# Delta-rule attention in front of two MoE layers: key-query products and state updates over four quarters of the array

## The chip, the cores and the metric

One core of one Trainium2 chip runs the whole program. The metric is the device time of one execution in microseconds. Three runs of the kernel before took 1043.93, 1046.31 and 1048.43 us; the median is 1046.31 us.

## The reference

Attention has 4 batches, 8 heads, 768 tokens and head size 48. Each head carries a 48x48 state that every token updates by a delta rule:

```python
k_n = k / (np.linalg.norm(k, axis=-1, keepdims=True) + 1e-06)
state = np.zeros((B, H, D, D), dtype=np.float32)
for t in range(S):
    kt, vt, bt = (k_n[:, :, t], v[:, :, t], beta[:, :, t, None])
    y[:, :, t] = np.einsum('bhd,bhde->bhe', q[:, :, t], state)
    v_old = np.einsum('bhde,bhd->bhe', state, kt)
    state = state + bt[:, :, :, None] * np.einsum('bhd,bhe->bhde', kt, vt - v_old)
```

The result, turned to 3072 tokens of 384 numbers, goes through two layers of the form `act(x @ w_in) @ w_out` with 2048 hidden units: an ELU in the first, `h * sigmoid(1.702 h)` in the second. All in float32.

## The kernel before, in words

**Chunks.** The tokens of a head are cut into 12 chunks of 64. Within a chunk the recurrence is solved in closed form: a Gram matrix of the keys (`gram`, L174) is inverted as a triangular system (`inverse`, `join16`, and `t2`, `m1`, `m2` in `chunk`), and the rest is small matrix products per head. `chunk(c)` (L331) returns these steps by name: `kq` (products of keys and queries, 64x64 per head, L352), `mask` (their strict causal part, L368), `ks` (keys times the old state, L414), `w` (the inverse applied to the values less that, L430), `state` (the new state, L451), `y` (the output, L464) and `out` (a transpose into the tiles that the first MoE layer reads, L486).

**Where the heads lie.** There are 32 pairs of batch and head. They are named by `hf` (0 or 1), `ab` (0 or 1) and `u` (0 to 7). `tok(ab)` is the partition half (0 to 63 or 64 to 127) in which the tokens of a head lie for `ks`, `w` and `y`. `w_half(hf, ab)`, called `k`, is `ab` for `hf` 0 and `1 - ab` for `hf` 1. The tiles `x[k]` and `su[k]` each hold two things: for `x[k]`, queries (48 rows) in half `1 - k` and the masked key-query products in half `k`; for `su[k]`, the state in half `1 - k` and the result of `w` in half `k`. So `y` is one product over all 128 partitions.

**Which part of the array a product uses.** The rows of the array are the partitions of the operands, its columns the partitions of the output. Before the change, `kq` reads half `1 - k` and writes half `k` (L359 to L365), and `state` reads half `k` and writes half `1 - k` (L456 to L459): both use two of the four quarters of 64x64, in turn by `turns()` (L105). `ks` reads half `1 - k` and writes half `ab` (L420 to L426), and `w` reads half `ab` and writes half `k` (L438 to L443), both by `order()` (L100).

**VectorE behind them.** `mask` (L377) multiplies the products, read from PSUM, by a 0/1 mask into `x[k]`: two operations of 64x1024 a chunk, or four of 64x512 for chunk 0, whose products lie in two separate PSUM tiles. `state` (L462) adds its product, read from PSUM, to the state into the other copy `nx[k]`: two operations of 48x768.

**Order of the work.** Everything is in program order on each engine. Chunks 0 and 1 run in a hand-written order ahead of the MoE work (L744 to L811). After that the program runs through units of the first MoE layer, 9 matmuls `up` (L576) and 9 matmuls `down` (L610) of 128x512 each; tables of slots (L829 to L867) say at which unit and at which of three places in it each step of a chunk is issued. `mask` is issued right behind its `kq` from chunk 2 on. A step costs the table a due share of VectorE (`VECTOR`, L943), which sets how the inverse of later chunks and the splitting of weights (`prep`, L541 to L555) are spread. All of `kq`, `ks`, `w`, `state`, `y`, `gram` and `out` take the one PSUM tile `ps_w` of two banks (`wide`, L118, one buffer), so each waits until the one before has been read out. In chunks 0 and 1 some take the banks of the MoE accumulators instead.

The DMA issues all stand on SyncE's queue, and none belongs to the changed steps.

Of the kernel before, what the change touches and what calls it, by code (L numbers as in the profile page):

```python
# [14 lines left out]
ALU = mybir.AluOpType  # L15
PSUM = bass.MemoryType.PSUM

B, H, S, D = 4, 8, 768, 48
# [9 lines left out]
HB = D * H  # L28
# [3 lines left out]
class Kernel:  # L32
# [67 lines left out]
    def order():  # L100

        return [(hf, ab) for hf in range(2) for ab in range(2)]

    @staticmethod
    def turns():  # L105

        return [(0, 0), (0, 1), (1, 1), (1, 0)]

    @staticmethod
    def tok(ab):  # L110
# [220 lines left out]
    def chunk(self, c):  # L331

        nc, ap = self.nc, self.ap
        v, pe, act, pool = nc.vector, nc.tensor, nc.scalar, nc.gpsimd
        first, last = c == 0, c == NC - 1
        s = self.pas[c // 2]
        us = slice(16 * (c % 2), 16 * (c % 2) + 16)
        su = [self.su[k, c % 2] for k in range(2)]
        nx = [self.su[k, 1 - c % 2] for k in range(2)]
        g = self.grp.setdefault(c, {})  # L340
        st = {}

        def hs(u):
            return slice(u * D, (u + 1) * D)
# [7 lines left out]
        def kq():  # L352
            if first:
                ps = self.banks(0)
            else:
                both = self.wide()
                ps = [both[:, hf] for hf in range(2)]
            for u in range(8):
                for hf, ab in self.turns():  # L359
                    k = self.w_half(hf, ab)  # L360
                    r = 64 * (1 - k)
                    pe.matmul(  # L362
                        ps[hf][self.tok(k), 64 * u:64 * u + 64], g["kt"][r:r + D, 8 * hf + u, :],
                        g["x"][k][r:r + D, 8 * hf + u, :], start=True, stop=True,
                    )  # L365
            st["kq"] = ps if first else both

        def mask():  # L368
            ps = st.pop("kq")
            for k in range(2):  # L370
                r = self.tok(k)
                for f, part in (((0, ps[0]), (1, ps[1])) if first else ((None, ps),)):
                    if f is None:
                        o, i = g["x"][k][r], part[r].rearrange("p f (u t) -> p (f u) t", u=8)
                    else:
                        o, i = g["x"][k][r, 8 * f:8 * f + 8], part[r].rearrange("p (u t) -> p u t", u=8)
                    v.tensor_tensor(  # L377
                        out=o, in0=i, in1=self.mask_p[r].unsqueeze(1).to_broadcast(list(i.shape)), op=ALU.mult,
                    )

        def t2():
            st["t2"] = self.place(c, "t2")
# [68 lines left out]
        def state():  # L451
            if last:
                return
            ps = self.wide()
            for u in range(8):
                for hf, ab in self.turns():  # L456
                    k = self.w_half(hf, ab)
                    t, r = self.tok(k), slice(64 * (1 - k), 64 * (1 - k) + D)
                    pe.matmul(ps[r, hf, hs(u)], g["kn"][t, hf, hs(u)], su[k][t, hf, hs(u)], start=True, stop=True)  # L459
            for k in range(2):  # L460
                r = slice(64 * (1 - k), 64 * (1 - k) + D)
                v.tensor_tensor(out=nx[k][r], in0=su[k][r], in1=ps[r, :, 0:HB], op=ALU.add)  # L462

        def y():  # L464
            st["y"] = ap.tile([P, 2, HB], F32, name="y", tag="ry", bufs=2)
# [20 lines left out]
        def out():  # L486
# [10 lines left out]
            for i in range(2):  # L497
# [4 lines left out]
                v.tensor_tensor(out=xl[:, :, dst], in0=src, in1=xh[:, :, dst].bitcast(F32), op=ALU.subtract)  # L502

        return dict(nv=nv, t2=t2, m1=m1, kq=kq, mask=mask, m2=m2, ks=ks, w=w, state=state, y=y, out=out)

    def x_tiles(self, key):
# [536 lines left out]
```

## Time and profile before

| what | value |
|---|---|
| runs | 1043.93, 1046.31, 1048.43 us |
| span of the profiled execution | 1047.7 us; no other time of this execution is given |
| TensorE busy | 996.2 us (95%), 12136 matmul rows |
| VectorE busy | 591.2 us (56%), 1021 instructions |
| ScalarE busy | 453.4 us (43%) |
| attention's work | from the start to about 570 us |

A product of two float32 operands shows as two matmul rows in the profile, so a step over 32 heads shows as x64 for one chunk. "PEld" is the weight load of TensorE, which runs beside its matmuls. "PEclk" is the granted TensorE clock in tenths of full speed. "Idle before" in square brackets is the time for which the engine stood idle ahead of that row, with what ended it; "issue" is a wait for nothing that the profile shows.

### The profile page before, as it was taken

Reading aid. Unit: us, or ns where it says so; the run is one execution under the profiler, and the core shown is the slowest. Engines: PE = TensorE matmul, PEld = TensorE weight load, DVE = VectorE, ACT = ScalarE, POOL = GpSimd, SP = SyncE. Lnnn points to the kernel's source line nnn. Section 1 sums busy time; section 2 is a strip of 40 time slices with the busy share of each in tenths; the row PEclk is TensorE's granted clock in tenths of the full one; section 3 lists DMA queues with packets and bytes.
Section 4 is the critical chain, followed back from the end, with each engine's and each line's share of the span. In section 5 each row is a group of like instructions: output and inputs, shape, how many; then the busy total and the mean of one; then the engine's idle time right before and its main releaser. Section 6 shows DMA issues by size and latency. Waiting matters only on the chain.

```text
span 1047.7 us, 26839 instructions
## 1 busy us (share of the span) xinstructions
PE 996.2 (95%) x12136; PEld 854.1 (82%) x12136; DVE 591.2 (56%) x1021; ACT 453.4 (43%) x749; POOL 49.5 (5%) x65
## 2 busy tenths in 40 slices
PE   2678898999999999999999999999999999999998
PEld 2666776877788888888888788999999999999997
DVE  5579568837786777668434676743333333333333
ACT  1254575544445445545544766533333333333322
POOL 2000000000001000000000010000100001000000
PEclk9677999999999999999999999999999999999999
DMA  5252341401220221211001741001010010010000
GB/s 178 114 174 97 114 153 53 132 34 61 63 91 20 72 77 53 71 39 65 18 17 61 281 201 61 1 1 61 1 53 9 1 61 1 23 38 1 31 1 31
DMA packets 20178, 68.40 MB, mean 65 GB/s; under 512 B 3168, under 2 KB 6240, under 8 KB 20064
## 3 DMA queue, kind: packets, MB, share of 16 engines
q1 hardware_dynamic: 20064, 66.69, 18.7%
q8 instruction: 95, 1.56, 0.6%
q14 instruction: 19, 0.16, 0.0%
HBM read 57.25 MB, written 9.44 MB: 64 GB/s over the span
## 4 chain that ended last, share of the span: by engine, by line
PE 92%; DVE 4%; issue 2%; DMA 1%; ACT 1%; SPq 0%; ACTq 0%; DVEq 0%
PE h L576 38%; PE acc L610 18%; PE acc L621 10%; PE accn L621 10%; PE ps_w L362 2%; PE ps_w L474 2%; PE ps_w L459 2%; PE ps_w L188 2%; PE ps_b L392 1%; PE ps_b L407 1%; PE ps_w L423 1%; DMA kg<-in_kT 1%; PE ps_w L440 1%; PE ps_w L496 1%; PE ps_b L323 1%
## 5 line engine op out<-in xcount | busy, mean ns | idle before, releaser
L576 PE MATMUL h<-xh,wt 128*128 128x512 f32 x1152 | 401.0, 402 | 6.4 <-DVE wt L555 5.0
L576 PEld LDWEIGHTS h<-xh,wt 128*128 128x128 f32 x1152 | 219.5, 191 | 53.2 <-DVE wt L555 6.3
L576 PE MATMUL h<-xl,wt 128*128 128x512 f32 x576 | 229.4, 398 | 0.0
L610 PE MATMUL acc<-gh,wt 128*128 128x512 f32 x576 | 197.0, 396 | 0.5 <-DVE xo L674 0.5
L598 ACT CAST gh<-t 128x512 fp32r<-128x512 f32 x192 | 119.2, 621 | 174.8 <-DVE t L589 118.7
L601 DVE TENSOR_TENSOR gl<-t,gh 128x512 fp32r<-128x512 f32 x192 | 138.7, 723 | 68.1 <-PE acc L621 30.9
L595 DVE TENSOR_TENSOR t<-t,h 128x512 f32<-128x512 f32 x96 | 66.0, 688 | 180.3 <-ACT t L592 180.2
L592 ACT ACTIVATE t<-h 128x512 f32<-128x512 f32 x96 | 57.4, 598 | 198.9 <-PE h L576 198.9
L610 PEld LDWEIGHTS acc<-gh,wt 128*128 128x128 f32 x576 | 108.9, 189 | 24.4 <-issue 0.9
L576 PEld LDWEIGHTS h<-xl,wt 128*128 128x128 f32 x576 | 109.8, 191 | 19.2 <-DVE xl L502 0.2
L610 PE MATMUL acc<-gl,wt 128*128 128x512 f32 x288 | 112.9, 392 | 0.0
L589 DVE SCALAR_TENSOR_TENSOR t<-t,h 128x512 f32<-128x512 f32 x96 | 65.6, 684 | 76.2 <-ACT t L586 75.7
L585 ACT ACTIVATE t<-h 128x512 f32<-128x512 f32 x96 | 57.4, 598 | 113.5 <-PE h L576 112.8
L621 PE MATMUL acc<-wt,gh 128*128 128x384 f32 x384 | 98.5, 337 | 0.0
L621 PE MATMUL accn<-wt,gh 128*128 128x384 f32 x384 | 98.1, 336 | 0.0
L621 PEld LDWEIGHTS accn<-wt,gh 128*128 128x128 f32 x384 | 71.0, 188 | 5.4
L621 PEld LDWEIGHTS acc<-wt,gh 128*128 128x128 f32 x384 | 70.3, 188 | 2.8
L621 PE MATMUL acc<-wt,gl 128*128 128x384 f32 x192 | 64.9, 338 | 0.0
L621 PE MATMUL accn<-wt,gl 128*128 128x384 f32 x192 | 64.8, 337 | 0.0
L610 PEld LDWEIGHTS acc<-gl,wt 128*128 128x128 f32 x288 | 54.4, 189 | 10.3
L586 ACT ACTIVATE t<-t 128x512 f32<-128x512 f32 x96 | 60.6, 632 | 3.0
L640 POOL TENSOR_TENSOR xl<-x1r,xh 128x512 fp32r<-128x512 f32 x18 | 24.4, 1355 | 413.9 <-ACT xh L639 321.8
(143 smaller groups left out, 968.7 us busy)
## 6 DMA issues: line engine op xcount, KB each, us to landing
raw<-in_w SPq DMA_DIRECT2D x32, 768.0 KB, 7.4
kt<-in_kT SPq DMA_DIRECT2D x12, 512.0 KB, 4.6
x<-in_qT SPq DMA_DIRECT2D x24, 256.0 KB, 4.2
kg<-in_kT SPq DMA_DIRECT2D x10, 512.0 KB, 4.7
vn<-in_vn SPq DMA_DIRECT2D x12, 384.0 KB, 4.3
kn<-in_kn SPq DMA_DIRECT2D x12, 384.0 KB, 3.6
x1d<-xo SPq DMA_DIRECT2D x12, 384.0 KB, 2.9
x1r<-x1d SPq DMA_DIRECT2D x6, 768.0 KB, 4.6
```

What stands on the lines that cost most here:

```text
L188: self.nc.tensor.matmul(o[q:q + 32], k[:, 32 * sub:32 * sub + 32], x, start=True, stop=True)
L576: nc.tensor.matmul(hps, wt[:, part, k * P:(k + 1) * P], src[:, k, c], start=(i == 0), stop=(i == 3 * NK - 1))
L585: nc.scalar.activation(out=t, in_=hps, func=AF.Relu, scale=-1.0)
L586: nc.scalar.activation(out=t, in_=t, func=AF.Exp, scale=-1.0)
L589: nc.vector.scalar_tensor_tensor(out=t, in0=t, scalar=-1.0, in1=hps, op0=ALU.add, op1=ALU.max)
L592: nc.scalar.activation(out=t, in_=hps, func=AF.Sigmoid, scale=1.702)
L595: nc.vector.tensor_tensor(out=t, in0=t, in1=hps, op=ALU.mult)
L598: nc.scalar.copy(gh, t)
L601: nc.vector.tensor_tensor(out=gl, in0=t, in1=gh.bitcast(F32), op=ALU.subtract)
L610: self.nc.tensor.matmul(acc[c], wt[:, part, DM + c * P:DM + (c + 1) * P], src, start=(m == 0 and i == 0), stop=(m == NM - 1 and i == 2),)
L621: self.nc.tensor.matmul(acc[w], src[:, c], wt[:, part, DM:2 * DM], start=(m == 0 and i == 0), stop=(m == NM - 1 and i == 2),)
L640: nc.gpsimd.tensor_tensor(out=xl, in0=raw, in1=xh.bitcast(F32), op=ALU.subtract)
```

## The change

`kq` writes half `ab` in place of half `k`, and `state` writes half `1 - ab` in place of `1 - k`; both go through the heads by `order()`. Operands stay where they were. So each of the two steps uses all four quarters of the array. For `hf` 1 the result now lies in the other partition half from where it belongs, and the VectorE operation that reads it from PSUM writes it to its half. As the halves of `hf` 0 and 1 no longer go together, `mask` and the state's addition become four operations each. `turns()` is gone.

```diff
--- before.py
+++ after.py
@@ -100,11 +100,6 @@
     def order():
 
         return [(hf, ab) for hf in range(2) for ab in range(2)]
-
-    @staticmethod
-    def turns():
-
-        return [(0, 0), (0, 1), (1, 1), (1, 0)]
 
     @staticmethod
     def tok(ab):
@@ -356,27 +351,24 @@
                 both = self.wide()
                 ps = [both[:, hf] for hf in range(2)]
             for u in range(8):
-                for hf, ab in self.turns():
+                for hf, ab in self.order():
                     k = self.w_half(hf, ab)
                     r = 64 * (1 - k)
                     pe.matmul(
-                        ps[hf][self.tok(k), 64 * u:64 * u + 64], g["kt"][r:r + D, 8 * hf + u, :],
+                        ps[hf][self.tok(ab), 64 * u:64 * u + 64], g["kt"][r:r + D, 8 * hf + u, :],
                         g["x"][k][r:r + D, 8 * hf + u, :], start=True, stop=True,
                     )
-            st["kq"] = ps if first else both
+            st["kq"] = ps
 
         def mask():
             ps = st.pop("kq")
-            for k in range(2):
-                r = self.tok(k)
-                for f, part in (((0, ps[0]), (1, ps[1])) if first else ((None, ps),)):
-                    if f is None:
-                        o, i = g["x"][k][r], part[r].rearrange("p f (u t) -> p (f u) t", u=8)
-                    else:
-                        o, i = g["x"][k][r, 8 * f:8 * f + 8], part[r].rearrange("p (u t) -> p u t", u=8)
-                    v.tensor_tensor(
-                        out=o, in0=i, in1=self.mask_p[r].unsqueeze(1).to_broadcast(list(i.shape)), op=ALU.mult,
-                    )
+            for hf, ab in self.order():
+                k, t = self.w_half(hf, ab), self.tok(ab)
+                i = ps[hf][t].rearrange("p (u t) -> p u t", u=8)
+                v.tensor_tensor(
+                    out=g["x"][k][self.tok(k), 8 * hf:8 * hf + 8], in0=i,
+                    in1=self.mask_p[t].unsqueeze(1).to_broadcast(list(i.shape)), op=ALU.mult,
+                )
 
         def t2():
             st["t2"] = self.place(c, "t2")
@@ -453,13 +445,14 @@
                 return
             ps = self.wide()
             for u in range(8):
-                for hf, ab in self.turns():
+                for hf, ab in self.order():
                     k = self.w_half(hf, ab)
-                    t, r = self.tok(k), slice(64 * (1 - k), 64 * (1 - k) + D)
+                    t, r = self.tok(k), slice(64 * (1 - ab), 64 * (1 - ab) + D)
                     pe.matmul(ps[r, hf, hs(u)], g["kn"][t, hf, hs(u)], su[k][t, hf, hs(u)], start=True, stop=True)
-            for k in range(2):
-                r = slice(64 * (1 - k), 64 * (1 - k) + D)
-                v.tensor_tensor(out=nx[k][r], in0=su[k][r], in1=ps[r, :, 0:HB], op=ALU.add)
+            for hf, ab in self.order():
+                k = self.w_half(hf, ab)
+                r, q = [slice(64 * (1 - x), 64 * (1 - x) + D) for x in (k, ab)]
+                v.tensor_tensor(out=nx[k][r, hf], in0=su[k][r, hf], in1=ps[q, hf, 0:HB], op=ALU.add)
 
         def y():
             st["y"] = ap.tile([P, 2, HB], F32, name="y", tag="ry", bufs=2)
```

## Rows read from the trace of the kernel before

**Rows 1.** The page, parts 1 and 2: busy time, and granted clock in 40 slices.
```profile
PE 996.2 (95%) x12136; PEld 854.1 (82%) x12136; DVE 591.2 (56%) x1021; ACT 453.4 (43%) x749; POOL 49.5 (5%) x65
...
PEclk9677999999999999999999999999999999999999
```

**Rows 2.** Stages: stretch, length, busy PE, PEld, DVE, ACT, POOL; clock, DMA share, GB/s.
```profile
0.00:75.00 75.00, 43.37 (x1804) 39.84 (x1804) 44.06 (x97) 22.88 (x41) 9.30 (x22) 0.82 0.48 157
75.00:179.00 104.00, 90.63 (x1881) 71.80 (x1882) 79.16 (x127) 57.27 (x97) 3.65 (x6) 0.90 0.33 109
179.00:570.00 391.00, 388.51 (x6121) 319.10 (x6122) 258.67 (x507) 183.89 (x303) 12.11 (x19) 0.99 0.18 55
570.00:1047.00 477.00, 473.72 (x2333) 423.38 (x2331) 209.30 (x292) 189.31 (x310) 24.39 (x18) 1.00 0.13 50
```

**Rows 3.** Timeline of TensorE, full clock: start, length, line, out<-in, shape, count.
```profile
364.48 1.64 PE L459 MATMUL ps_w<-su,kn 64*48 64x48 f32 x64
...
375.11 2.08 PE L362 MATMUL ps_w<-x,kt 48*64 48x64 f32 x64
...
396.57 1.49 PE L188 MATMUL ps_w<-kg 48*32 48x64 f32 x128
...
422.09 1.15 PE L423 MATMUL ps_w<-su,kt 48*64 48x48 f32 x64
...
428.60 1.15 PE L440 MATMUL ps_w<-r,z 64*64 64x48 f32 x64
```

**Rows 4.** Timeline of VectorE: masks, state additions, and copies of half the width.
```profile
45.84 2.57 DVE L377 TENSOR_TENSOR x<-acc,mask_p 64x512 f32<-64x512 f32 x4
...
61.32 1.92 DVE L462 TENSOR_TENSOR su<-su,ps_w 48x768 f32<-48x768 f32 x2 [2.17 <-PE ps_w L459]
...
69.54 1.12 DVE L447 COPY su<-acc 64x384 f32<-64x384 f32 x2 [0.54 <-PE acc L440]
```

**Rows 5.** Waits by total, count and longest; then timeline rows of the PSUM buffer.
```profile
DVE x L377 <- PE ps_w L362: 16.3, 10, 3.0
DVE su L462 <- PE ps_w L459: 16.0, 10, 3.0
...
238.39 1.15 PE L423 MATMUL ps_w<-su,kt 48*64 48x48 f32 x64 [0.38 <-DVE x L377]
...
377.24 2.47 DVE L377 TENSOR_TENSOR x<-ps_w,mask_p 64x1024 f32<-64x1024 f32 x2 [1.11 <-PE ps_w L362]
...
381.43 2.07 PE L474 MATMUL ps_w<-su,x 128*64 128x48 f32 x64
```

**Rows 6.** TensorE before 100 us: three bursts, and the stage of one.
```profile
54.75 1.95 PE L440 MATMUL acc<-vn,z 64*64 64x48 f32 x62 [0.24 <-ACT z L412]
...
58.47 2.80 PE L459 MATMUL ps_w<-su,kn 64*48 64x48 f32 x64
...
94.13 3.68 PE L362 MATMUL ps_w<-x,kt 48*64 48x64 f32 x64
...
94.00:98.00 4.00, 4.00 (x66) 3.75 (x66) 2.91 (x5) 1.95 (x3) 0.00 (x0) 0.50 0.86 291
```

**Rows 7.** The chain of waits (start, length, what), and a DMA queue of the page.
```profile
34.80 1.84 issue
...
123.75 1.78 PE ps_w L362 x56
125.53 0.86 issue
...
q8 instruction: 95, 1.56, 0.6%
```

**Rows 8.** Timeline of TensorE and VectorE where VectorE's chain comes between.
```profile
90.85 1.22 PE L576 MATMUL h<-xh,wt 128*128 128x512 f32 x2 [3.68 <-DVE wt L555]
...
152.21 1.92 DVE L462 TENSOR_TENSOR su<-su,ps_w 48x768 f32<-48x768 f32 x2 [1.26 <-PE ps_w L459]
...
178.93 1.51 PE L496 MATMUL ps_w<-ident,y 128*128 128x128 f32 x6 [2.64 <-DVE su L462]
```

## The prediction, made before the change was run

> **What bounds the kernel now.** I read the page first. TensorE is busy 95% of the span, and its granted clock is at the upper of its two levels (2.4 GHz) in most slices after the first fifth [rows 1]. A kernel like that gets shorter by what TensorE no longer has to do, but only in stretches where TensorE is what ends last. So I then cut the span into stages [rows 2]. From 179 to 570 us TensorE is busy 388.5 of 391 us, VectorE 258.7: here TensorE alone sets the pace. From 75 to 179 us TensorE is busy 90.6 of 104 us and VectorE 79.2: the two take turns. Before 75 us TensorE is busy 43.4 of 75 us: waits rule. After 570 us the attention is over and nothing of the change runs.
>
> The third view is the timeline of TensorE at the full clock, where a burst is read off whole [rows 3]. All bursts below have 64 matmul rows (32 products, two rows each), except the Gram product with 128. The two that the change touches are the slow ones: the key-query burst takes 2.08 us and the state burst 1.64 us, both in two quarters of the array. The key-state product (L423) and the w product (L440) take 1.15 us; their code goes through all four quarters, L423 in the very order that the changed key-query products take. So the trace of before already holds the changed form's price. There are 12 key-query bursts (chunks 0 to 11) and 11 state bursts (chunks 0 to 10).
>
> **TensorE's part.** The key-query product keeps its 64 stationary columns, as L423 has them, and streams 64 columns where L423 streams 48. The Gram product streams 64 too and needs only 1.49 us for 128 rows [rows 3], so the streamed columns do not seem to set the pace. I take 1.15 us; the bad end is 1.15 x 64/48 = 1.53 us. Saved: 0.93 us a burst (0.55 to 0.93). The state product has 48 stationary columns, between the Gram product's 32 (1.49/128 = 11.6 ns a row) and L423's 64 (18.0 ns). Halfway is 14.8 ns, so 0.95 us (ends: 0.75 and 1.15). Saved: 0.69 us (0.49 to 0.89).
>
> **The order against the rule.** The changed order within a unit visits the row halves as B, A, A, B, so every second row has its predecessor in the same half. L440 goes A, B, A, B and L423 goes B, A, A, B, and both take 1.15 us [rows 3]: the order costs nothing there. The Trainium skill, "TensorE: Matmul & The Clock Gate", Part 3 (Packing small matmuls), says that a weight load overlaps running matmuls only when it goes to another row group. By that rule about half of the loads would be exposed, and the sum below would be about half as large; the equal rows speak against it.
>
> **VectorE's part.** Two masks of 64x1024 become four of 64x512. The first chunk has that form already: four in 2.57 us, against 2.47 us for two wide ones [rows 4]. That adds 0.10 us a chunk. Two state additions of 48x768 (1.92 us) become four of 48x384. The nearest row is a pair of 64x384 copies from PSUM at 1.12 us, so four take 2.24 us: 0.32 us more. New is also that half of these operations write to the partition half that they don't read from. No row shows that. I take no extra cost, because the nearest rows are the same shapes within a half. It may not gain, since the element count per partition is unchanged; as its bad end I take four times the time, which is the third rival below. In the stage after 179 us the extra time is covered: VectorE mostly stands waiting for just these bursts, 10 times each for 16.3 and 16.0 us [rows 5], so it begins earlier when they end earlier. And the single PSUM buffer that mask and addition must free is next wanted later: the mask that starts at 377.24 ends at 379.71, while the next user starts at 381.43 [rows 5]. Where VectorE is the bound, the cover is gone and the 0.10 or 0.32 us counts. Chunk 0's mask has four operations either way. No DMA is moved and the program order of the pieces stays.
>
> **The sum, burst by burst.**
> - After 179 us, 8 key-query bursts (chunks 4 to 11) and 7 state bursts (chunks 4 to 10): 8 x 0.93 + 7 x 0.69 = 12.3 us. At chunk 4 the key-state product already waits 0.38 us for the mask [rows 5], so the mask's 0.10 us counts there.
> - Key-query of chunk 2, at 94 us, runs at the lower clock level (0.50 granted in 94 to 98 us) and takes 3.68 us. The w product at that level takes 1.95 us for 62 rows, 2.0 us for 64 [rows 6]. TensorE works on without waiting behind it, so 1.7 us are saved.
> - State of chunk 0, at 58 us, takes 2.80 us at the lower level [rows 6]; I take 1.8 us, so 1.0 us is saved (0 to 1.2). Behind it TensorE has work in a row.
> - Key-query of chunks 0 and 1: nothing (0 to 2.8 us). They are followed by a stall of 1.84 us in which TensorE waits for nothing that the profile shows [rows 7]. Such stalls come back after each 128 or so dense matmuls with as many weight loads. The queue of kind "instruction" carries 95 packets in 1.56 MB [rows 7], 16.4 KB each. I read this as code arriving in blocks; the block that ends that stall would not come sooner because TensorE ran out of the previous one sooner. Key-query of chunk 3 is broken by such a stall after 56 of its rows [rows 7]: nothing either (0 to 0.9).
> - State of chunk 1: VectorE follows it and TensorE waits 3.68 us for the weights that VectorE splits [rows 8]. The burst's gain goes into that wait, and VectorE's addition lies on the path: a loss of about 0.15 us.
> - State of chunks 2 and 3: the addition of chunk 2 starts right behind the burst, and from there VectorE is the chain until TensorE has waited 2.64 us for the addition of chunk 3 [rows 8]. Gained 0.69 at the head, lost 0.32 twice, and the second burst's gain ends in the wait: nothing.
>
> Together: 12.3 - 0.1 + 1.7 + 1.0 - 0.15 = 14.7 us. The profiled span is 1047.7 us; its execution has no separate time, so I count nothing around the span. It lies 1.4 us above the median of the runs, 1046.31, and inside their spread. 1047.7 - 14.7 = 1033.0, and against the median 1031.6; I forecast 1032 us.
>
> **The rivals.**
> - Half of it. Successive rows in one row half block each other, so half run at the pace of the two-quarter burst. Key-query 1.62 us, state 1.30 us: 8 x 0.46 + 7 x 0.34 + 1.3 for the early ones less 0.25 = 7.2 us, so 1039 us. For it: I infer the mechanism of the slow pace from few shapes, and none is 64 by 64 in four quarters. Against it: L423 and L440 [rows 3]. Chance 0.13. The skill's rule above is this rival.
> - The change doesn't do what it says: the quarters still run one after the other for these operands. Then only VectorE's additions count, 0.32 three times and 0.10 once, so 1047 us. Chance 0.06.
> - Slower: writing to the other partition half is slow on VectorE. If such an operation takes four times the others' 0.64 and 0.56 us, a mask takes 6.4 us and an addition 5.6 us. Between the burst's end and the next user of the buffer some 4.2 us pass [rows 5], so four masks would stall TensorE 2.2 us each, chunk 4's about 3.9, seven additions 1.4 each, and the three additions on VectorE's own stretches [rows 8] add 3.7 each: 33.6 us against 14.7 gained, 1065 us. At three times it costs 16.5 us and breaks even; from there it decides. Nothing in the trace speaks for or against it but the steady price per element of all VectorE rows. Chance 0.05.
> - More: the early key-query bursts gain as well, since the code blocks are asked for earlier: 14.7 + 2.8 + 0.9, so 1028 us. Chance 0.06.
>
> **How the numbers follow.** The forecast keeps 0.70. Its own range: with 1.53 us for key-query and 1.15 us for state, and nothing at chunk 0, the gain is 9 us; with 0.75 us for state and the early bursts, 20 us: 1026 to 1037 us. The runs of before lie 2 us to either side of their median. With the half rival the range is 1025 to 1040 us. About 0.5% (5.2 us) is what a measurement of this kernel can tell from no change; faster than 1041 us are the forecast, the greater gain and most of the half rival: 0.87. Same: the quarters that don't overlap and the rest: 0.08. Slower: 0.05.
>
> **What would show it.** In the profile after, the key-query burst at 1.15 us and the state burst near 0.95 us at the full clock; four masks in about 2.6 us and four additions in about 2.25 us, those that cross halves as long as the others; TensorE's busy time in the stage after 179 us down by some 12 us with no new waits on L377 or L462; the stalls at 35 and 125 us still there and longer; the wait for the addition of chunk 3 still near 2.6 us. The prediction is wrong if the bursts keep a pace above 25 ns a row, if crossing operations are longer, or if new waits of TensorE of over a microsecond drop its clock to the lower level where it was at the upper.

## The result and the profile after

The changed kernel takes 1035.78 us (median of four runs, 1033.48 to 1037.44) against 1046.57 us for the kernel before in the same session (median of four, 1043.93 to 1048.43). Over all these runs the ratio is 0.9893, 95% interval 0.9872 to 0.9914. Run again as it is, beside other kernels, it came to 0.9882 (0.9860 to 0.9905). So it is 11 to 12 us faster. The forecast was 1032 us, 14.7 us faster; the range of 1025 to 1040 us held.

The page of the profiled execution, its span and part 1, to be read against [rows 1]:

```profile
span 1035.7 us, 26881 instructions
...
PE 982.5 (95%) x12136; PEld 837.4 (81%) x12136; DVE 598.6 (58%) x1065; ACT 453.2 (44%) x749; POOL 49.2 (5%) x65
```

TensorE has as many matmuls as before and is busy 13.7 us less. VectorE has 44 instructions more (two more masks and two more additions for each of 11 chunks) and 7.4 us more to do.

Line numbers move with the diff: L362 is now L357, L377 is L368, L459 is L451, L462 is L455. TensorE's bursts at the full clock, in the timeline (start, length, line, out<-in), against [rows 3]:

```profile
359.82 0.94 PE L451 MATMUL ps_w<-su,kn 64*48 64x48 f32 x64
...
369.74 1.16 PE L357 MATMUL ps_w<-x,kt 48*64 48x64 f32 x64
```

The state burst went from 1.64 to 0.94 us and the key-query burst from 2.08 to 1.16 us.

VectorE's new operations, first all of a line (count, shortest/median/longest in ns), then one group of four in the timeline for each, against [rows 4]:

```profile
L368 DVE TENSOR_TENSOR x<-ps_w,mask_p x44: 676/690/695, 50.3 to 547.1; 64x512 f32<-64x512 f32 x44
...
L455 DVE TENSOR_TENSOR su<-su,ps_w x44: 545/553/558, 58.7 to 515.4; 48x384 f32<-48x384 f32 x44
...
370.97 2.80 DVE L368 TENSOR_TENSOR x<-ps_w,mask_p 64x512 f32<-64x512 f32 x4 [0.20 <-PE ps_w L357]
...
427.79 2.25 DVE L455 TENSOR_TENSOR su<-su,ps_w 48x384 f32<-48x384 f32 x4 [0.95 <-PE ps_w L451]
```

In each group of four, the last two write to the other partition half. In the mask group shown the four last 684, 695, 683 and 695 ns, and between the shortest and the longest of a line lie 19 and 13 ns. So an operation that crosses is not longer than one that doesn't.

Four masks take 2.80 us (2.47 before), four additions 2.25 us (1.92 before). Not all of that is the cutting into four. The kernel called VectorE's split only, described below, has the same shapes, all within their own half, and its groups are shorter:

```profile
373.96 2.62 DVE L377 TENSOR_TENSOR x<-ps_w,mask_p 64x512 f32<-64x512 f32 x4 [1.10 <-PE ps_w L362]
...
432.38 2.05 DVE L463 TENSOR_TENSOR su<-su,ps_w 48x384 f32<-48x384 f32 x4 [1.64 <-PE ps_w L459]
```

There two masks of one half follow each other, and the second starts 0.61 us after the first, before that has ended; where the half changes it is 0.70 us. In the changed kernel the half that is read changes with every operation, and every step is 0.70 to 0.71 us, also between the first two, neither of which crosses. So about 0.2 us of each group goes by the order of the operations, not by the crossing.

The waits in total, against the first two of [rows 5]:

```profile
DVE su L455 <- PE ps_w L451: 9.1, 9, 2.3
DVE x L368 <- PE ps_w L357: 7.6, 9, 2.7
PE ps_w L489 <- DVE su L455: 3.6, 1, 3.6
PE ps_w L415 <- DVE x L368: 0.7, 1, 0.7
```

VectorE stood 16.3 and 16.0 us waiting for these bursts; now it is 7.6 and 9.1 us. That idle time is what the added instructions and the shorter bursts were taken from. TensorE's own waits for them grew from 2.64 to 3.65 us at the addition of chunk 3 and from 0.38 to 0.74 us at the mask of chunk 4.

**Where the 12 us came from.** One mark that all kernels share is the start of chunk 4's key-query burst. In the profile before, then after:

```profile
233.66 2.08 PE L362 MATMUL ps_w<-x,kt 48*64 48x64 f32 x64
```

```profile
233.58 1.16 PE L357 MATMUL ps_w<-x,kt 48*64 48x64 f32 x64
```

Up to there the two profiled executions are level. From there to the end of the span it is 1047.7 - 233.66 = 814.0 us before and 1035.7 - 233.58 = 802.1 us after: 11.9 us, all of it behind the mark.

### The profile page after: what moved, and what is told of

The parts are those of the page before. It is cut to its first block, busy times and chain, and to the rows that moved or that the text cites. A ratio compares the mean times of both kernels' runs of the same rounds, so it can differ in the third digit from the quotient of the medians.

```text
span 1035.7 us, 26881 instructions
## 1 busy us (share of the span) xinstructions
PE 982.5 (95%) x12136; PEld 837.4 (81%) x12136; DVE 598.6 (58%) x1065; ACT 453.2 (44%) x749; POOL 49.2 (5%) x65
## 4 chain that ended last, share of the span: by engine, by line
PE 90%; DVE 5%; issue 2%; DMA 1%; ACT 1%; SPq 0%; ACTq 0%
PE h L569 39%; PE acc L603 19%; PE acc L614 10%; PE accn L614 10%; PE ps_w L467 2%; PE ps_w L357 1%; PE ps_w L183 1%; PE ps_b L399 1%; PE ps_b L384 1%; PE ps_w L415 1%; PE ps_w L432 1%; PE ps_w L451 1%; PE ps_w L489 1%; PE ps_b L310 1%; PE ps_b L318 1%
```

## The experiments

Three questions were open: do the late bursts carry the whole gain; what became of the 1.7 + 1.0 - 0.15 = 2.55 us forecast for the chunks before 179 us; and why are four quarters faster. In the table, "rest" is the span less the start of chunk 4's key-query burst, and the ratio is that to the kernel before, run in the same session.

| kernel | ratio and 95% interval | burst of chunk 4 starts | rest |
|---|---|---|---|
| before (profile shown above) | 1 | 233.66 | 814.0 |
| changed | 0.9893 (0.9872 to 0.9914) | 233.58 | 802.1 |
| changed, again | 0.9882 (0.9860 to 0.9905) | 232.02 | 801.9 |
| key-query only | 0.9933 (0.9909 to 0.9957) | 235.37 | 807.5 |
| state only | 0.9965 (0.9946 to 0.9984) | 231.08 | 808.8 |
| VectorE's split only | 1.0013 (0.9997 to 1.0029) | 230.69 | 813.8 |
| chunks 4 to 11 only | 0.9878 (0.9861 to 0.9895) | 232.19 | 801.9 |
| chunks 0 to 3 only | 1.0012 (0.9996 to 1.0028) | 233.58 | 814.4 |
| chunk 3's key-query as before | 0.9875 (0.9855 to 0.9895) | 229.49 | 802.4 |
| chunk 3's key-query moved | 0.9880 (0.9854 to 0.9906) | 226.68 | 801.8 |
| row halves alternate | 0.9879 (0.9858 to 0.9899) | 231.94 | 802.2 |

**The parts.** Key-query only keeps the old state update, state only the old key-query products and masks:

```diff
 def kq():
-  for hf, ab in self.turns():  ... ps[hf][self.tok(k), ...]
+  for hf, ab in self.order():  ... ps[hf][self.tok(ab), ...]
```

> Only the key-query products take four quarters and four masks; the state update stays as before. Theory A: 8 bursts after 179 us save 0.92 us each, 7.4 us, and the early chunks lose about 2 us through the longer stall and the clock: 1040 to 1042 us. Rival V (VectorE's added instructions eat the gain): under 3 us gained, over 1043 us, with new waits of TensorE for the mask beyond the one of chunk 4.

Measured: 0.9933, 7 us of the 1046.57; the rest is 6.5 us shorter. In the forecast's terms it should be 8 x 0.92 less the 0.36 us that the mask of chunk 4 costs, 7.0 us; the missing 0.5 us was not traced. Rival V, under 3 us gained, is out.

```diff
 def state():
-  for hf, ab in self.turns():  ... slice(64 * (1 - k), 64 * (1 - k) + D)
+  for hf, ab in self.order():  ... slice(64 * (1 - ab), 64 * (1 - ab) + D)
```

> Only the state update takes four quarters and four additions; the key-query products stay as before. Theory A: 7 bursts after 179 us save 0.70 us each, 4.9 us, chunk 0 up to 1 us, and chunk 3's key-query stall stays at 0.9 us without a fall of the clock: 1040 to 1042 us. Rival V (VectorE's added instructions eat the gain): over 1043.5 us, with longer waits of TensorE for the additions.

Measured: 0.9965, 3.7 us (1.7 to 5.7); the rest is 5.2 us shorter, against 7 x 0.70 = 4.9. The median is 1042.96 us beside 1048.39 us for the kernel before in that session, and the interval reaches into the expected gain of 4.6 to 6.6 us without covering it. The late part is as expected; what the early part gave can't be told from these runs. The two parts' rests add to 11.7 us, the changed kernel's 11.9.

**VectorE's share alone.** The products stay in two quarters, and masks and additions are only cut into four:

```diff
-  for f, part in (((0, ps[0]), (1, ps[1])) if first else ((None, ps),)):
+  for f, part in ((0, ps[0]), (1, ps[1])):
...
-  v.tensor_tensor(out=nx[k][r], in0=su[k][r], in1=ps[r, :, 0:HB], op=ALU.add)
+  for hf in range(2):
+      v.tensor_tensor(out=nx[k][r, hf], in0=su[k][r, hf], in1=ps[r, hf, 0:HB], op=ALU.add)
```

> Both products stay in two quarters as before; only VectorE's masks and additions are split into four, all within their own half. This is VectorE's part of the change alone. Theory A: the extra 0.3 us an addition and 0.3 us a mask are hidden but for chunks 1 to 4: 0 to 1.5 us slower than before, 1046 to 1048 us. Rival V: 3 us or more slower, 1049 to 1051 us.

Measured: 1.0013 (0.9997 to 1.0029), and a rest of 813.8 us, as before. The cost is hidden in the late stretch. In all, the interval runs from 0.3 us faster to 3.0 us slower, so Rival V is just at its end. The operations of this kernel stay in their half, so it does not hold the 0.2 us a group that the changed order adds.

**The early chunks.** The profile after shows the key-query burst of chunk 3 cut by a stall, as in [rows 7], and a slow stretch behind it. First the burst in the timeline, then pieces of the chain of waits (start, length, what), then the stretch as a whole (as in [rows 2], the clock is the third number from the end):

```profile
121.15 1.04 PE L357 MATMUL ps_w<-x,kt 48*64 48x64 f32 x56
...
123.88 0.49 PE L357 MATMUL ps_w<-x,kt 48*64 48x64 f32 x8 [1.69 <-issue]
```

```profile
124.38 4.14 PE acc L603 x9
...
130.36 3.81 PE h L569 x9
...
135.30 2.28 PE acc L603 x9
```

```profile
124.00:134.00 10.00, 10.00 (x90) 7.56 (x90) 6.97 (x10) 2.77 (x5) 0.00 (x0) 0.52 0.10 16
```

The 56 rows ahead of the stall went from 1.85 to 1.04 us, and the stall from 0.86 to 1.69 us: what the burst saved, the stall took. Then nine long matmuls took 4.14 and 3.81 us, where at the upper clock level they take 2.28. Before, this stretch ran at the upper level. The first theory was therefore that the longer stall drops the clock, and that this is the missing time. Three kernels were run to see it.

> The changed kernel once more, unaltered. Theory A: in the changed kernel the key-query burst of chunk 3 runs out of instructions sooner, the stall behind its 56th row grows from 0.9 to 1.7 us, and TensorE's granted clock falls behind it, which costs about 4 us. Then the stall of some 1.7 us at 122 us and the lower clock in 124 to 134 us come back, and the time is 1034 to 1037 us. Theory B: the fall of the clock there was chance of one execution; then the clock is at the upper level in 124 to 134 us in this one, and its span is some 4 us shorter than 1035.7.

The same kernel again, burst and stretch:

```profile
123.69 1.04 PE L357 MATMUL ps_w<-x,kt 48*64 48x64 f32 x56
...
126.37 0.34 PE L357 MATMUL ps_w<-x,kt 48*64 48x64 f32 x8 [1.63 <-issue]
```

```profile
124.00:134.00 10.00, 8.37 (x208) 6.70 (x200) 7.21 (x11) 4.89 (x10) 0.00 (x0) 1.00 0.23 83
```

The stall is there again at 1.63 us, and the clock stayed up. So the longer stall belongs to the change, and the fall of the clock behind it does not come every time. Theory B called it chance of one execution, but the kernels below show it too. Here is the same stretch of the kernel with chunks 0 to 3 only in the new form, then of the one with chunks 4 to 11 only, where this burst is as before:

```profile
124.00:134.00 10.00, 8.34 (x178) 6.61 (x166) 6.85 (x11) 4.33 (x8) 0.00 (x0) 0.83 0.24 83
```

```profile
124.00:134.00 10.00, 10.00 (x161) 7.91 (x160) 7.33 (x9) 5.39 (x10) 0.00 (x0) 0.85 0.17 51
```

Their stalls are 1.66 and 1.13 us. Over the profiles in which this burst is cut, the stall is 0.58 to 1.13 us with two quarters (five profiles) and 1.63 to 3.55 us with four (seven). Behind it the clock of this stretch is below 1.00 in one of the five and in five of the seven; with a stall of 1.66 us it is 0.83 in one kernel and 1.00 in another. So the longer stall goes with more falls, in few executions of each.

The span of the second execution is only 1.8 us shorter than that of the first, not the 4 us of theory B.

```diff
-  for hf, ab in self.order():  ... ps[hf][self.tok(ab), ...]
+  for hf, ab in ([(0, 0), (0, 1), (1, 1), (1, 0)] if c == 3 else self.order()):  ... ps[hf][self.tok(k if c == 3 else ab), ...]
```

> Only chunk 3's key-query products go back to two quarters (VectorE's four masks stay). Theory A: the stall in the burst is 0.9 us again, the clock stays at the upper level, and the kernel is about 4 us faster than the changed one although this burst is 0.9 us longer: 1031 to 1033 us. Theory B (the fall of the clock has nothing to do with the burst): 0 to 1 us slower than the changed one, 1036 to 1037 us.

Measured: 1034.54 us, ratio 0.9875; the stall is 0.86 us again in its profile, and the clock stayed up. The 4 us did not come: the interval overlaps most of the changed kernel's, and the two medians of the session, 1034.54 and 1035.28 us, lie 0.7 us apart.

```diff
-  (10, 3, "kq"), (10, 3, "mask"), (11, 2, "m2"),
+  (11, 2, "m2"), (11, 3, "kq"), (11, 3, "mask"),
```

> Chunk 3's key-query products and mask are issued one slot later, behind the 32x32 products m2 of chunk 2 and a unit of long matmuls, not right behind the 256 instructions of the join. Theory A: no stall over 0.5 us around that burst, no lower clock behind it: 1030 to 1032 us, 4 to 6 us faster than the changed kernel. Theory B: the same time as the changed kernel, 1034 to 1037 us.

Measured: 0.9880, though its profiled execution was the shortest of all with a span of 1028.5 us and an unbroken burst of 1.16 us. Its runs went from 1030.29 to 1039.53 us. One profile of this kernel's early stretch says little about its mean. Neither kernel without the long stall is measurably faster, so the theory of the clock does not explain the whole of the missing time; that it takes a part of it, in some executions, is neither shown nor ruled out.

So the early chunks were taken by themselves. `four` stands for the changed form, the other branch is that of before:

```diff
+  four = c >= 4
...
+  if four:
...
+  else:
```

> Four quarters only from chunk 4 on; chunks 0 to 3 as before. Theory E (the early chunks give nothing on average: what their bursts save, they lose again in stalls for code, in VectorE's chain and to the clock): 12 us faster than before, the same as the changed kernel within its 2 us. Rival F (the early chunks cost time in the changed kernel): faster than the changed kernel by 2 us or more. Rival G (they gain the 2.4 us of the forecast): 2.4 us slower than the changed kernel.

```diff
+  four = c < 4
```

> Four quarters only in chunks 0 to 3; the others as before. Theory E: the time of before, within 1.5 us, ratio 0.9985 to 1.0015. Rival F: slower than before by 2 us or more. Rival G: 2.4 us faster than before, ratio 0.9977. In all cases the stretch behind the first key-query burst of chunk 4 takes 814 us as before.

Measured: 0.9878 (0.9861 to 0.9895) for the late chunks alone, and 1.0012 (0.9996 to 1.0028) for the early ones alone, 1.3 us slower with 0.4 us faster still inside. The late ones alone give as much as the whole change. A gain of 2.4 us in the early chunks (rival G) lies outside the interval. Theory E (within 1.5 us) and rival F (2 us or more lost) can't be told apart: the interval holds both, with its middle in E. So the early chunks gained nothing, and may have lost up to some 3 us. The starts of chunk 4's burst in the table go from 226.68 to 235.37 us, in no order by the form of the early bursts.

The profiles also show where the forecast's largest early term goes. It was the key-query burst of chunk 2, in the profile after:

```profile
93.73 1.99 PE L357 MATMUL ps_w<-x,kt 48*64 48x64 f32 x64
```

It took 3.68 us before, so the burst did shrink by 1.7 us. But the time from its start to the start of chunk 3's key-query burst is 29.6 us in the profile before, 26.8 to 27.2 us in three other kernels with the old form there, and 27.4 to 28.3 us in six with the new form. The mean granted clock of this stretch is 0.84 in the profile before, 0.91 to 0.95 in the other three, and 0.83 to 0.91 in the six. What the clock does there from one execution to the next weighs as much as the burst.

**Why four quarters are faster.** Here the order within a unit is changed, so that successive rows lie in different row halves:

```diff
-  for hf, ab in self.order():
+  for hf, ab in [(0, 0), (0, 1), (1, 1), (1, 0)]:
```

> The changed kernel with the heads of a unit in another order, so that successive rows of TensorE always lie in different row halves (A, B, A, B instead of B, A, A, B). If the row halves of neighbours don't matter, the bursts stay at 1.16 and 0.94 us and the time within 2 us of the changed kernel, 1034 to 1037 us. If a weight load is hidden only behind a matmul in the other row half, the bursts get shorter, to 0.9 and 0.7 us or so, and the kernel is 3 to 4 us faster, 1031 to 1033 us.

```profile
335.96 0.94 PE L451 MATMUL ps_w<-su,kn 64*48 64x48 f32 x64
...
368.14 1.16 PE L357 MATMUL ps_w<-x,kt 48*64 48x64 f32 x64
```

The bursts are equal to 10 ns, and the ratio is 0.9879. The Trainium skill, "TensorE: Matmul & The Clock Gate", Part 3 (Packing small matmuls), has a weight load overlap matmuls only in another row group. The trace does not show that here: in these bursts, where the quarter changes with every row, 1.16 and 0.94 us come out whether the neighbour lies in the same row half or not.

```diff
-  for u in range(8):
-      for hf, ab in self.order():
+  for hf, ab in self.order():
+      for u in range(8):
```

> The changed kernel with the four quarters one after the other: 16 rows in the first quarter, then 16 in the next. If a quarter takes one row after the other, load and stream in turn, each row takes twice the pace of two quarters: 63 ns for key-query and 49 ns for state, so bursts of 4.0 and 3.1 us at the full clock, and the kernel is slower than before by 8 x 1.9 + 7 x 1.5 = 26 us or more, 1070 to 1080 us. If the pace hangs on the instruction count alone, the bursts stay at 1.16 and 0.94 us.

```profile
382.83 2.66 PE L451 MATMUL ps_w<-su,kn 64*48 64x48 f32 x64
...
394.51 3.40 PE L357 MATMUL ps_w<-x,kt 48*64 48x64 f32 x64
```

One run, 1081.78 us. With the same matmuls, loads and operands the bursts take 3.40 and 2.66 us, not the 4.0 and 3.1 expected, and not the 1.16 and 0.94 of the same instruction count. So the count of instructions does not set the pace; the quarters do. The rest is 835.8 us, 21.8 more than before, of which the bursts are 8 x 1.32 + 7 x 1.02 = 17.7.

How they do it can be read from the starts of single rows, which the trace holds and the timeline merges:

| form | key-query: rows 5 to 8 ns apart, time from one such group to the next | state |
|---|---|---|
| one quarter at a time | 1 row, 58 ns | 1 row, 45 ns |
| two quarters in turn (before) | 2 rows, 58 ns | 2 rows, 45 ns |
| four quarters (changed) | 4 rows, 58 ns | 4 rows, 45 ns |

In every form a quarter starts one row each 58 or 45 ns, and the quarters run beside each other. So each doubling of the quarters doubles the pace: about 58, 29 and 15 ns a row, and 45, 23 and 11. The bursts with one quarter at a time are shorter than 64 x 58 and 64 x 45 ns because the last three rows of a quarter run beside the first three of the next. L423 and L440 of the kernel before, with 64 stationary columns and 48 streamed ones, have groups of four each 58 ns too. So the time of a quarter follows the stationary columns in these rows (64: 58 ns, 48: 45 ns), not the streamed ones.

**Towards a better kernel.** VectorE's chain from 153 to 180 us ends in TensorE's wait of 3.65 us, in the profile after:

```profile
180.73 0.85 PE L489 MATMUL ps_w<-ident,y 128*128 128x128 f32 x6 [3.65 <-DVE su L455]
```

The next two kernels begin the inverse of chunks 4 and 5 two units later, the second also issues chunk 4's key-query products a slot earlier:

```diff
-  self.passes(at, spread, end, fill, p, (3, 6), (9, o + 2), lambda: turned(2))
+  self.passes(at, spread, end, fill, p, (3, 6), (11, o + 2), lambda: turned(2))
```

> The changed kernel, with the inverse of chunks 4 and 5 begun two units later. In the changed kernel VectorE is the chain from 153 to 180 us and TensorE waits 3.7 us for chunk 3's state addition; the inverse's first steps stand ahead of it on VectorE. If that wait is set by VectorE's queue: the wait goes to under 1 us, the lower clock behind it goes too, and the kernel is 3 to 5 us faster than the changed one, 1030 to 1032 us, unless the inverse then ends too late for chunk 4 at about 215 us. If not: 1034 to 1037 us.

```diff
-  (10, a, "kq"), (11, a, "ks"),
+  (9, a, "kq"), (11, a, "ks"),
```

> As inv_later, and chunk 4's key-query products and mask one slot earlier, so that four masks have 4.5 us in place of 2.3 us before the key-state product wants the PSUM buffer. TensorE's wait of 0.74 us for the mask at 237 us goes: 0.7 us faster than inv_later. If the mask is not what it waits for, the same time as inv_later.

TensorE's row behind the addition of chunk 3, in the profile with the later inverse:

```profile
179.07 0.85 PE L489 MATMUL ps_w<-ident,y 128*128 128x128 f32 x6 [0.80 <-DVE su L455]
```

The wait fell from 3.65 to 0.80 us, as VectorE's queue would have it, but the ratios are 0.9876 (0.9848 to 0.9903) and 0.9883 (0.9861 to 0.9905). The profile with the later inverse has two waits behind it that the changed kernel's has not:

```profile
PE acc L603 <- DVE gl L594: 1.3, 1, 1.3
PE ps_w L489 <- ACT z L189: 0.9, 1, 0.9
```

They take back 2.2 of the 2.85 us. In the second the wait for chunk 4's mask is gone, and a new stall of 0.78 us without a releaser cuts that burst. No version here is measurably better than the changed kernel.

## Why the prediction was right, and where it was too high

- **Burst lengths.** Forecast 1.15 and 0.95 us, measured 1.16 and 0.94. Taking the price of the new form from L423, which had it already, was right: its rows start in the same groups of four. The halfway value for 48 stationary columns was partly luck, since the Gram product's rows, its lower end, do not start in such groups.
- **After 179 us.** The sum gave 12.3 - 0.1 us. The profile gives 11.9 us behind the mark at chunk 4, and the two parts alone 6.5 and 5.2. This is the whole of the measured gain, within its interval.
- **VectorE.** The masks were mis-sized: 2.80 us for four, not the 2.57 of chunk 0's row, so 0.33 more and not 0.10. Chunk 0's row had its masks in pairs of one half; the new order has not. It showed in one place, the wait of chunk 4, where 0.38 became 0.74 us. The additions came out as forecast (2.25 us), but by luck: kept in their half, four take 2.05 us. The fear of slow writes across halves was groundless.
- **Early chunks.** Here the sum failed. "So 1.7 us are saved" at the key-query of chunk 2 and "1.0 us is saved" at the state of chunk 0 should have left 2.55 us in the end; chunks 0 to 3 alone measure 1.3 us slower (0.4 us faster to 2.9 us slower). The step that failed is "TensorE works on without waiting behind it": the bursts did shrink, from 3.68 to 1.99 us and from 2.80 to 1.53 us, but the stretch behind chunk 2's is not shorter than in three kernels with the old burst. (The profile shows a clock of 1.00 during the 1.53 us; but chunk 1's state burst has the same length at 0.50.) What took the time back is shown in part. The stall behind the key-query bursts of chunks 0 and 1 grew from 1.84 to 2.65 us and the one at chunk 3 from 0.86 to 1.63 and 1.69 us, as forecast; the latter is what the burst ahead of it saves. The wait for chunk 3's addition grew by 1.0 us. That wait was named in the text as the place where the second burst's gain ends, so to expect it to stay near 2.6 us was a slip. How much the clock's falls and the loads of the start take on average is not settled.
- **A sign of being wrong that showed.** "New waits of TensorE of over a microsecond drop its clock": in the first profile after, the stall of 1.69 us at chunk 3 is followed by 0.52 granted where it was 1.00 before. Behind the mark at chunk 4 the longest wait of TensorE is 0.74 us, and there the sum was right.
- **The rivals.** Half of it and no overlap are refuted by the burst lengths, slow crossing writes by VectorE's rows. The greater gain from the earliest bursts did not come: chunks 0 to 3 alone gain at most 0.4 us.
- **The range.** It held because the late term, five sixths of the sum, was read from rows of the same form in a stretch where TensorE had no other wait.

## What to carry to other kernels

If a kernel already has an operation in the form that a change wants, its row is the price, and the sum is that price times the count in the stretch where the engine is the only bound. Ask also whether that row has its operations in the order that the change gives them, as the masks show. In a start-up stretch where several things take turns in ending last, count a shorter burst as nothing until something shows otherwise, and measure that stretch by itself: a common mark late in the program (here the first burst of chunk 4) parts a steady difference of 0.5 us from a start that scatters by over 8. When small products use only part of the array, the partition half of the output is a free choice if VectorE can bring the result home while it reads it from PSUM; its operations are then better ordered so that neighbours stay in one half, which no run here tried together with the change.

## What was not expected of the hardware

- A quarter starts a row each 58 ns (key-query, 64 stationary columns) or 45 ns (state, 48), whether one, two or four quarters are in use. One quarter at a time had been expected to give bursts of 4.0 and 3.1 us; 3.40 and 2.66 came, because neighbouring quarters overlap by three rows where they meet.
- Two VectorE operations in a row on the same partition half overlap by some 0.09 us; where the half changes from one to the next they do not. A group of four in alternating halves takes 0.2 us longer, crossing or not.
- A stall of 1.6 to 1.7 us at the same place was followed by the lower clock level for some 10 us in one execution of the changed kernel and by none in the other.
- With the wait for VectorE taken from 3.65 to 0.80 us, the kernel did not get measurably faster.
